# Corner clears moved from Pool to VectorE, output stores moved from SyncE to ScalarE, in a fused attention and expert-layer kernel

## The chip, the cores and the metric

The kernel runs on one core of a Trainium2 chip. The metric is the device time of one execution in microseconds (us). "Span" is the length of one execution inside its trace; it is about 1.8 us shorter than the time.

Each core has TensorE (matmuls; its weight loads are listed apart as PEld), VectorE (DVE), ScalarE (ACT), GpSimd (POOL) and SyncE (SP, which here only issues DMA transfers). Each gets its own list of instructions, and the timelines below show them carried out in that order.

## The reference

Causal block attention over 8 batches, 8 heads, 576 positions of width 64, with blocks of 64; then an expert layer with an activation that has a parameter for each hidden column.

```python
def _attn_ref(q, k, v):                       # (8, 8, 576, 64) each
    scores = scale * np.matmul(q, k.transpose(0, 1, 3, 2))
    # ... mask: a query's block of 64 sees its own block and the earlier ones
    attn = np.exp(scores - max)               # cut
    attn = attn / (np.sum(attn, axis=-1, keepdims=True) + 1e-09)
    return np.matmul(attn, v)

def _moe_ref(x, w_in, w_out, beta):           # x (4608, 512), w_in (512, 2048), w_out (2048, 512)
    h = x @ w_in
    g = h * (1.0 / (1.0 + np.exp(-beta * h)))
    return g @ w_out
```

## The kernel before

The kernel doesn't write its instructions down in order. It hands operations to a small planner: engine, assumed duration in ns, function that emits it, what it depends on, which buffers it uses, and a priority. The planner simulates the engines with those durations and so fixes one order for each engine; then semaphores are given out and each engine's list is emitted. An operation that changes its engine, or its assumed duration, can therefore change the order of everything.

```python
P.schedule()          # list scheduling: fixes P.order["PE"], ["ACT"], ["DVE"], ["POOL"], ["SP"]
P.assign(None)        # semaphores
# ...
def emit(self, e, eng, sems):
    for o in self.order[e]:
        for n, v in o.waits:
            eng.wait_ge(sems(n), v)           # the whole queue of the engine stands here
        ins = o.emit(eng, e)
        # ...
```

A pair of heads makes three large exponentials on ScalarE, and after each one a 64x64 corner that the causal mask forbids has to be set to zero in both heads. Scores are stored with the key on the partition axis, so a corner lies in partitions 64 to 127. Attention times V waits for these clears.

```python
x = P.op("ACT", act_t(1024), fe, deps=[o], tiles=[ps, te], ...)       # exponential, line 560
def fz(g, e, g0=g0, te=te):
    if g0 < 2:
        return g.memset(E3[te.slot][64:128, g0, :, 0:64], 0.0)        # line 566, 64 times
    # ... the third one: two corners in each head
    return g.memset(bass.AP(...), 0.0)                                # line 568, 32 times
zs.append(P.op("POOL", 200, fz, deps=[x], tiles=[te], prio=-40))
# ...
av = P.op("PE", 30 * 34, fav, deps=ex + zs + [load[u]], ...)          # attention times V, line 595
```

Pool also casts V of a batch from float32 to bf16 (line 441, `Vn<-Vs`), casts Q and K (lines 484 and 523), and issues the loads of `w_in` (line 396) and `w_out` (line 401), all in one queue. SyncE issues the loads of Q, K and V (V is lines 427 and 430), the transposing transfers (lines 530 and 625), and the stores:

```python
x = P.op(("ACT", "DVE"), 600, fv2, deps=[o], tiles=[po, to], lat=680, prio=0)      # scale by 0.5, line 722
def fd(g, e, to=to, row=row, w=w):
    return [g.dma_start(out[row + 128 * w:row + 128 * w + 128, :], ost[to.slot][:])]  # line 728
P.op("SP", 400, fd, deps=[x], tiles=[to], xfer=900, dma=["d_ost", to], prio=0)
```

The expert layer is lines 680 (matmuls of the first layer), 690 (tanh), 694 (multiply) and 711 (matmuls of the second layer), in nine chunks of 512 tokens. While the first scores aren't there yet, TensorE runs throwaway matmuls (line 411).

The softmax here doesn't subtract the row's maximum and nothing guards it: scores larger than these inputs give would overflow.

## Time and profile before

| | before |
|---|---|
| time, median of the first 3 runs | 370.88 us (369.81 to 371.85) |
| span of the profiled run | 369.8 us, mean granted TensorE clock 0.995 |
| busy: TensorE / ScalarE / VectorE / Pool | 343.9 / 209.1 / 156.6 / 96.8 us |

The views that show what bounds the kernel stand in the prediction, with their reading. The groups of the two clears on Pool (count, busy time, mean ns of one, then Pool's idle time ahead of them), and the row of the stores among the DMA issues (size, then us from issue to landing):

```profile
L566 POOL MEMSET E<- 64x128 bf16 x64 | 13.1, 205 | 85.9 <-ACT E L560 83.8
L568 POOL MEMSET E<- 64x256 bf16 x32 | 9.8, 307 | 37.3 <-ACT E L560 36.1
...
out_dram<-ost SPq DMA_DIRECT2D x36, 256.0 KB, 2.2
```

96 clears are 23 us of work, in front of which Pool stands 123 us. And the busy time by engine in the two microseconds after the wait for the V cast that the prediction points at; the number after the engines is the granted clock:

```profile
56.00:58.00 2.00, 2.00 (x41) 2.00 (x38) 0.32 (x3) 0.00 (x0) 0.31 (x2) 0.50 1.21 195
```

TensorE is counted as fully busy there, at half speed.

### The profile page before, as it was taken

To read this page: it belongs to the slowest core of one execution; us is meant where nothing else is said; L and a number is where in the kernel's file an instruction comes from. 1 tells how busy PE (TensorE), PEld (TensorE's weight loads), DVE (VectorE), ACT (ScalarE), POOL (GpSimd) and SP (SyncE) were. 2 spreads that over 40 slices of the span, in tenths; PEclk is the share of its full clock that TensorE was granted. 3 is DMA by queue.
4 is the path that set the end of the run, shared out by engine and by line. 5 is a ranking of instruction groups with operands and counts; after the bars stand their busy time and mean duration, and the time that the engine had idled before them with its cause. 6 is when DMAs were issued, how large, how long until landed. Compare 5 with 4: busy or idle time off the path is not lost.

```text
span 369.8 us, 6994 instructions
## 1 busy us (share of the span) xinstructions
PE 343.9 (93%) x2755; PEld 176.0 (48%) x2797; DVE 156.6 (42%) x342; ACT 209.1 (57%) x308; POOL 96.8 (26%) x198
## 2 busy tenths in 40 slices
PE   7979969999898898998999999899999999999986
PEld 5656527544444544554544444345544444444432
DVE  1565954056412664325751246215631730730710
ACT  1573793138627788539875599219823832733711
POOL 6565173103605606405505331501000000000000
PEclk9999998999999999999999999999999999999999
DMA  8999999198898998998968799582112002002002
GB/s 194 220 190 268 205 188 152 43 214 195 173 231 201 203 191 188 208 222 197 194 125 183 190 183 202 124 160 76 32 46 86 1 30 79 6 30 83 2 30 85
DMA packets 146529, 52.06 MB, mean 141 GB/s; under 512 B 134704, under 2 KB 141888, under 8 KB 146496
## 3 DMA queue, kind: packets, MB, share of 16 engines
q1 hardware_dynamic: 139872, 46.82, 56.8%
q0 software_dynamic: 4224, 4.19, 7.1%
q10 hardware_dynamic: 2400, 0.59, 0.9%
q8 instruction: 22, 0.36, 0.4%
q14 instruction: 11, 0.09, 0.1%
HBM read 36.71 MB, written 9.44 MB: 125 GB/s over the span
## 4 chain that ended last, share of the span: by engine, by line
PE 78%; ACT 12%; DVE 4%; issue 3%; POOL 2%; POOLq 0%
PE PS L711 34%; PE PS L680 28%; ACT E L560 8%; PE PS L595 7%; ACT th L690 3%; PE PS L552 3%; PE PS L411 3%; DVE gT L694 2%; PE PS L637 2%; POOL Vn L441 1%; DVE xq L613 1%; ACT ost L722 1%; PE PS L493 1%; ACT E L572 0%; DVE xT L644 0%
## 5 line engine op out<-in xcount | busy, mean ns | idle before, releaser
L694 DVE SCALAR_TENSOR_TENSOR gT<-th,PS 128x512 bf16<-128x512 f32 x144 | 97.5, 685 | 105.8 <-ACT th L690 105.5
L680 PE MATMUL PS<-xT,w_in 128*128 128x512 bf16 x554 | 127.8, 379 | 3.0 <-DVE xT L644 0.6
L711 PE MATMUL PS<-w_out,gT 128*128 128x512 bf16 x556 | 125.8, 379 | 4.2 <-DVE gT L694 2.6
L690 ACT ACTIVATE th<-PS,beta 128x512 f32<-128x512 f32 x144 | 98.7, 707 | 33.8 <-PE PS L680 33.8
L560 ACT ACTIVATE E<-PS 128x1024 bf16<-128x1024 f32 x96 | 96.0, 1061 | 18.0 <-PE PS L552 17.8
L711 PEld LDWEIGHTS PS<-w_out,gT 128*128 128x128 bf16 x576 | 54.9, 98 | 68.6 <-DVE gT L694 3.7
L680 PEld LDWEIGHTS PS<-xT,w_in 128*128 128x128 bf16 x576 | 53.2, 98 | 64.8 <-DVE gT L694 2.1
L722 ACT ACTIVATE ost<-PS 128x512 f32<-128x512 f32 x35 | 20.9, 597 | 101.9 <-PE PS L711 101.9
L552 PE MATMUL PS<-QKT 64*64 64x64 bf16 (+5 forms) x384 | 36.9, 281 | 5.3 <-ACT E L560 3.7
L595 PE MATMUL PS<-Vn,E 128*128 128x65 bf16 x960 | 35.6, 196 | 5.4 <-POOL Vn L441 2.2
L523 POOL CAST QKn<-ST 128x640 bf16<-128x640 f32 x48 | 34.6, 721 | 14.6 <-DMA ST<-in_k_dram 7.4
L595 PEld LDWEIGHTS PS<-Vn,E 128*128 128x128 bf16 x960 | 32.8, 99 | 11.3 <-issue 3.4
L566 POOL MEMSET E<- 64x128 bf16 x64 | 13.1, 205 | 85.9 <-ACT E L560 83.8
L605 DVE RECIPROCAL inv<-PS 128x5 f32<-128x5 f32 x64 | 8.3, 173 | 49.1 <-PE PS L595 49.0
L613 DVE TENSOR_TENSOR xq<-PS,inv 128x320 bf16<-128x320 f32 x64 | 28.5, 486 | 0.0
L552 PEld LDWEIGHTS PS<-QKT 64*128 64x128 bf16 (+1 forms) x384 | 13.5, 95 | 29.9 <-issue 11.2
L441 POOL CAST Vn<-Vs 128x2560 bf16<-128x2560 f32 (+1 forms) x9 | 18.7, 2082 | 22.2 <-DMA Vs<-in_v_dram 21.5
L644 DVE COPY xT<-PS 128x64 bf16<-128x64 bf16 (+2 forms) x44 | 10.7, 287 | 29.2 <-PE PS L637 29.2
L568 POOL MEMSET E<- 64x256 bf16 x32 | 9.8, 307 | 37.3 <-ACT E L560 36.1
L411 PE MATMUL PS<-identF,identB 128*128 128x256 bf16 x104 | 15.8, 310 | 2.2 <-POOL identF L355 2.2
L501 DVE COPY QKT<-PS 128x576 bf16<-128x576 bf16 x16 | 11.7, 752 | 8.3 <-PE PS L493 8.3
L411 PEld LDWEIGHTS PS<-identF,identB 128*128 128x128 bf16 x104 | 10.9, 111 | 5.1 <-POOL identF L355 2.2
(29 smaller groups left out, 63.6 us busy)
## 6 DMA issues: line engine op xcount, KB each, us to landing
out_dram<-ost SPq DMA_DIRECT2D x36, 256.0 KB, 2.2
Vs<-in_v_dram SPq DMA_DIRECT2D x28, 256.0 KB, 4.0
ST<-in_q_dram SPq DMA_DIRECT2D x48, 128.0 KB, 2.8
ST<-in_k_dram SPq DMA_DIRECT2D x48, 128.0 KB, 2.7
ST<-in_q_dram SPq DMA_DIRECT2D x8, 288.0 KB, 7.9
ST<-in_k_dram SPq DMA_DIRECT2D x8, 288.0 KB, 7.9
w_in<-in_moe_w_in_dram POOLq DMA_DIRECT2D x4, 512.0 KB, 6.8
w_out<-in_moe_w_out_dram POOLq DMA_DIRECT2D x4, 512.0 KB, 9.3
```

The source lines that it names most:

```text
L411: return g.matmul(PS[:, tf.slot, 0:256], identB[:], identW)
L441: return g.tensor_copy(Vn[t.slot][:, :, h0:h1, 0:64], Vs[ts.slot][:, :, h0:h1, :])
L523: return g.tensor_copy(QKn[tn.slot][:].rearrange("p a w n -> p (a w n)")[:, 640 * (2 * a + w):][:, 0:640] .rearrange("p (t h d) -> p t h d ...
L552: z = g.matmul(o, QKT[tqk.slot][r, p, 1, 128 * t:128 * t + m], QKT[tqk.slot][r, p, 0, q0:q1])
L560: return g.activation(E3[te.slot][:, g0, :, :], PS[:, ps.slot:ps.slot + 2, :], ACT.Exp, scale=0.125)
L595: z = g.matmul(o, eblk(te, t, i, h), Vn[Tv.slot][:, t, 2 * c + h, 0:65], start=(t == 0), stop=(t == i))
L613: return g.tensor_tensor(xq[tx.slot][:, :, 64 * w:64 * w + 64], a, x, ALU.mult)
L680: z = g.matmul(PS[:, ph.slot, :], w_in[:, c, 128 * j:128 * j + 128], xT[:, c, row % RX:row % RX + RC], start=(c == 0), stop=(c == 3))
L690: return g.activation(th[tt.slot][:], PS[:, ph.slot, :], ACT.Tanh, scale=beta[:, j:j + 1])
L694: return g.scalar_tensor_tensor(out=gT[tg.slot][:, j, :], in0=th[tt.slot][:], scalar=1.0, in1=PS[:, ph.slot, :], op0=ALU.add, op1=ALU.mult)
L711: z = g.matmul(PS[:, po.slot, :], gT[tg.slot][:, j, 128 * w:128 * w + 128], w_out[:, j, :], start=(j == 0), stop=(j == NJ - 1))
L722: return g.activation(ost[to.slot][:], PS[:, po.slot, :], ACT.Copy, scale=0.5)
```

## The change

Its intent: Pool and SyncE each carry a kind of instruction that mostly waits for ScalarE, and everything behind it in the same in-order queue waits along. The clears go to VectorE. The scaling of an output tile goes to ScalarE always, and ScalarE then issues the store itself.

```diff
-                    zs.append(P.op("POOL", 200, fz, deps=[x], tiles=[te], prio=-40))
+                    zs.append(P.op("DVE", 160 if g0 < 2 else 220, fz, deps=[x], tiles=[te], prio=-20))
 ...
-                x = P.op(("ACT", "DVE"), 600, fv2, deps=[o], tiles=[po, to], lat=680, prio=0)
+                x = P.op("ACT", 600, fv2, deps=[o], tiles=[po, to], lat=680, prio=0)
 ...
-                P.op("SP", 400, fd, deps=[x], tiles=[to], xfer=900, dma=["d_ost", to], prio=0)
+                P.op("ACT", 500, fd, deps=[x], tiles=[to], xfer=900, dma=["d_ost", to], prio=-1)
```

## The prediction

> **What bounds the kernel now.** I read the engine table first, then the stages (busy time in chosen stretches), then the waits of every engine and of the SyncE queue, and last the instructions in order of time around the gaps of TensorE.
>
> ```profile
> PE 343.9 (93%) x2755; PEld 176.0 (48%) x2797; DVE 156.6 (42%) x342; ACT 209.1 (57%) x308; POOL 96.8 (26%) x198
> DMA  8999999198898998998968799582112002002002
> ```
> TensorE is the bound: 343.9 of 369.8 us, 25.9 us idle. The DMA row shows a second limit: the 16 DMA engines are full for about the first 60 us.
>
> ```profile
> 0.00:32.00 32.00, 27.50 (x341) 19.80 (x342) 15.42 (x41) 13.17 (x17) 17.93 (x49) 1.00 1.07 212
> 32.00:60.00 28.00, 24.35 (x216) 13.24 (x218) 17.91 (x32) 19.64 (x29) 12.78 (x21) 0.94 1.12 207
> 270.00:350.00 80.00, 79.63 (x365) 36.32 (x371) 30.82 (x45) 37.96 (x57) 0.00 (x0) 1.00 0.12 42
> ```
> The columns are the stretch, its length, busy time of TensorE, its weight loads, VectorE, ScalarE and Pool, granted clock, DMA share and GB/s. The idle time is not even: 4.5 us before 32, 3.65 us in 32 to 60, 12.7 us in 60 to 270 (the attention and the expert layer interleaved), 0.4 us in the 80 us of expert layer alone. The last 19.8 us hold 4.7, of which about 3 are the last scaling and store. The group of throwaway matmuls of the fill (104, 15.8 us in records that overlap; their starts are 0.11 us apart) hides another 11 us of emptiness before 32 us. So only the first 270 us can give anything, and at most some 35 us.
>
> ```profile
> POOL E L566 <- ACT E L560: 83.8, 40, 9.4
> POOL E L568 <- ACT E L560: 36.1, 23, 9.5
> PEld PS L595 <- POOL E L568: 0.8, 3, 0.3
> SPq L728 <- ACT ost L722: 110.5, 21, 18.9
> ```
> These are waits: total, times, longest. Pool stands 120 us before the corner memsets, and the SyncE queue 110 us before the output stores. But TensorE waits for a memset itself only 0.8 us. Any gain must therefore come from what stands behind them in the same in-order queues.
>
> ```profile
> 10.15 0.82 POOL L484 CAST QKn<-ST 96x768 bf16<-96x768 f32 x1 [2.28 <-DMA ST<-in_k_dram]
> 13.95 0.20 POOL L566 MEMSET E<- 64x128 bf16 x1 [2.98 <-ACT E L560]
> 14.49 0.87 POOL L396 DMA_DIRECT2D w_in<-in_moe_w_in_dram  x1 [0.34 <-POOL E L566]
> ...
> 18.59 0.82 POOL L484 CAST QKn<-ST 96x768 bf16<-96x768 f32 x1
> ...
> 46.19 0.20 POOL L566 MEMSET E<- 64x128 bf16 x1 [8.26 <-ACT E L560]
> ...
> 53.17 0.20 POOL L566 MEMSET E<- 64x128 bf16 x1 [1.18 <-ACT E L560]
> 53.43 2.32 POOL L441 CAST Vn<-Vs 128x2560 bf16<-128x2560 f32 x1
> ```
> This is Pool in order of time; the bracket is the idle time before. Two harms are visible. The K of the third head pair was issued at 3.6 us and landed 9.1 us later, at 12.7, yet is cast at 18.59: the weight load was issued late, behind a memset, and casts queue behind both. ScalarE then idles 2.13 us until the third pair's scores (its exponential starts at 21.54). And batch 1's V was issued by 43.3 us and had landed by 46.6, yet is cast at 53.43, behind memsets.
>
> ```profile
> 55.80 3.42 PE L595 MATMUL PS<-Vn,E 128*128 128x65 bf16 x60 [2.25 <-POOL Vn L441]
> ```
> TensorE pays 2.25 us for it, and then runs these 60 matmuls in 3.42 us where 30 take 1.01 us elsewhere; the granted clock of 55.8 to 59.3 is 0.54. That is another 1.4 us.
>
> **What the Trainium skill says.** "VectorE: DVE Perf Modes", section on zero memsets, states that a memset takes one cycle per element whatever the type. The trace agrees for float32: VectorE's own 64x256 memset takes 272 ns, against 267 for 256 cycles of 0.96 GHz. "SBUF — State Buffer", section "Who interferes with whom", says that a VectorE instruction with at most one SBUF input outside the 2-port modes doesn't contend with GpSimd; the trace of before cannot test it for these memsets. "DMA: Bandwidth & Descriptors", "Issuing engines are not separate DMA queues", says issuing from more engines saves only the sequencer's issue time, since the same 16 engines move the data. "Perfetto Trace Analysis", "DMA Instruction — HWDGE", puts the semaphore wait on the issuing sequencer ahead of the issue: the wait is what holds SyncE here, 110.5 us, where an issue itself takes 0.36 us in the median.
>
> **The change part by part.**
>
> Memsets. Pool loses 64 of 205 ns and 32 of 307 ns, 13.1 + 9.8 = 22.9 us, and with them the 120 us of waiting. VectorE gains, by one cycle per element (an estimate from the page above and the 272 ns row), 64 x 0.14 + 32 x 0.27 = 17.6 us: 156.6 becomes 174 us, 47%. It is far from a bound. The memset still follows its exponential, now in VectorE's queue, where it can meet a 0.69 us multiply (row 694) in front. As VectorE's multiplies follow ScalarE's tanh, in ScalarE's own order, a memset waiting for an exponential blocks little that could have run. I set +0.3 us.
>
> Pool freed, first stretch: the K cast can run near its landing, so the third pair's scores can follow the second's. I take the 2.1 us idle of ScalarE as gained; the first expert matmul (31.98 us, after the fourth pair's last copy) comes that much earlier. -2.1 us.
>
> Pool freed, 53 to 59: the V cast could run from 46.6 and end before 49. Removable are 2.25 + 1.4 = 3.65 us. The DMA engines are full here, and w_out issued earlier competes with V, so I credit three quarters: -2.8 us.
>
> Stores. SyncE loses 36 issues and the 110 us. The longest block is 18.9 us, from 53 to 71.85: the remaining V of batch 2 is issued at 73.95 and 79.98 and Pool waits 17.4 us for it, while DMA is at a 0.29 share in 60 to 70. TensorE does not idle then, having expert work (29.16 of 30 us in 60 to 90). The benefit can come only later, in the 12.7 us idle of 60 to 270, whose named waits are mainly on exponentials and multiplies, not loads. I credit an eighth: -1.5 us.
>
> ScalarE gains 36 issues. Its own queue issued four loads in 2.16 us at the start, 0.54 us each: 36 x 0.54 = 19 us, invisible as busy time. It must also wait for its own scaling to complete before the store. Twelve fall after 270 us, where it is busy 37.96 of 80 us: free. Of the other 24 only those in stretches where ScalarE is full count (10.00 of 10 us in 210 to 220): at most four, of which half meet a wait for TensorE. 2 x 0.54, +1.0 us. One scaling that VectorE did (679 ns) goes to ScalarE (597 ns): nothing.
>
> End: the last scaling ends at 367.26, SyncE issues at 367.28, the span ends 2.5 us later. ScalarE issuing it itself changes at most 0.1 us.
>
> Sum: +0.3 - 2.1 - 2.8 - 1.5 + 1.0 = -5.1 us, 370.88 - 5.1 = 365.8 us.
>
> **The rivals.** (a) The first 60 us belong to DMA: share 1.07 and 1.12. Then earlier casts only meet later data, and w_out and V trade places; the gain there falls to about 1 us and the time is 369. Against it: both named late casts had data waiting for 6 us. (b) The kernel plans its instruction order at build time from assumed durations, so the change reorders everything. If Pool, SyncE and their loads stay close to plan, the gaps at 93 to 97, 113 to 123 and 140 to 145 us, where attention runs without expert work between, could close as well: half of 12.7 us gives another 5, about 360. For it: batch 2's scores start only at 88.7 us, after 27 us almost without attention. Against it: TensorE's order is a plan's result, and the plan never saw these blocks. (c) ScalarE becomes the bound of the mixed stage: 99 of 145 us busy in 125 to 270 plus stores and their waits. If every one of the 24 stores delayed an exponential by 0.6 us that TensorE waits for, 14 us would be added and the time would be 375 or more. The 101.9 us that scalings wait for TensorE speak against it. (d) VectorE blocks: a memset in its queue that waits for an exponential holds the reciprocals and copies of the previous pair, and TensorE's chain turns around more slowly: +3 us, 369.
>
> **Range and chances.** My sum has large uncertain credits, and a new plan alone can move some microseconds either way. The range is 360.5 to 370.5 us, with (b) at the low end and (a) or (d) at the high one. The 2% line is 363.5 us: 2.3 us below my figure, within reach of (b): chance of faster 0.34. Within 2%: 0.60. Slower than 378.3 needs (c) in full or a bad plan: 0.06.
>
> **What would show it.** Right: Pool's waits for exponentials gone, about 72 to 75 us busy; the third pair's exponential near 19.4 us; first expert matmul near 30 us; no TensorE wait for the V cast near 53 and no clock near half there; SyncE's wait for scalings gone and no DMA hole at 60 to 70; 80 us of expert work alone unchanged near the end; VectorE near 174 us. Wrong: new TensorE waits on VectorE memsets, ScalarE stretches at 100% holding stores with TensorE idle beside them, memset rows longer than 0.3 us, or a first expert matmul still at 32 us. If the gain lies mostly in 60 to 270 us, rival (b) was the real mechanism and my two head terms were not.

## The result, and the profile after

| | before | after |
|---|---|---|
| median of 4 runs each | 370.35 us (369.29 to 371.85) | 366.76 us (366.54 to 367.03) |
| ratio | | 0.990, 95% interval 0.986 to 0.994: the same, by the 2% line |
| span of the profiled run, clock | 369.8 us, 0.995 | 364.7 us, 1.000 |

A ratio is the mean time of one kernel's fast runs over that of the other's in the same rounds, so it is not quite the ratio of the medians.

The kernel is faster by about 1%, and its runs scatter less. The engine rows:

```profile
PE 346.0 (95%) x2797; PEld 174.3 (48%) x2797; DVE 169.7 (47%) x437; ACT 209.2 (57%) x309; POOL 74.4 (20%) x102
```

(The 2.1 us more that TensorE seems to be busy can be a matter of records: in the trace of before 42 of its 2797 matmuls are missing, as its row in the prediction shows.) The stages, to be laid beside those of before:

```profile
0.00:32.00 32.00, 26.59 (x337) 19.30 (x338) 17.50 (x52) 13.17 (x17) 15.38 (x37) 1.00 1.10 222
32.00:60.00 28.00, 26.56 (x265) 13.84 (x264) 21.14 (x50) 22.09 (x32) 11.93 (x14) 1.00 1.14 204
270.00:350.00 80.00, 78.50 (x365) 35.44 (x363) 30.86 (x45) 37.41 (x56) 0.00 (x0) 1.00 0.11 40
```

The first stage has not gained. The second has TensorE busy 2.2 us longer at full clock instead of 0.94.

A better ruler than stages is how far TensorE has come. The expert matmuls have 1152 weight loads (9 chunks of 128), all of them in both traces. Reading the start of the n-th one in each trace and subtracting gives a ledger: where it steps, time was gained or lost.

```
n-th weight load of the expert matmuls   before     after     after - before
0                                          31.98     32.35      +0.37
64                                         59.84     57.15      -2.69
128                                        78.25     75.60      -2.65
384                                       164.69    162.00      -2.69
512                                       205.88    203.19      -2.69
576                                       228.71    225.37      -3.34
640                                       246.31    240.78      -5.52
736                                       274.78    269.67      -5.11
1151 (the last)                           366.03    360.92      -5.11
```

(Between the 384th and the 512th the two kernels run attention and expert work in another order, so the difference swings there and comes back.) Two steps make the whole gain: 3.06 us between 32 and 60 us, and 2.4 us between 205 and 275 us. Nothing was gained in the first 32 us, and nothing in the 145 us between the steps.

**The first step.** Pool's cast, then the first matmuls that use it (the x30 are one head pair; a bracket would show idle time before them), then the stretch with TensorE's clock:

```profile
51.11 2.32 POOL L441 CAST Vn<-Vs 128x2560 bf16<-128x2560 f32 x1 [9.28 <-DMA Vs<-in_v_dram]
```
```profile
53.64 1.08 PE L595 MATMUL PS<-Vn,E 128*128 128x65 bf16 x30
```
```profile
56.00:58.00 2.00, 2.00 (x30) 1.13 (x27) 2.00 (x8) 1.10 (x2) 0.23 (x1) 1.00 1.02 204
```

V of batch 1 is cast at 51.11 instead of 53.43 us, and attention times V follows its scores without idle time. The 2.25 us wait and the half clock after it are gone together. Note the bracket: Pool now waits 9.28 us for V to land. Before, the data was there and Pool was late; now Pool is early and the data sets the time. The data itself comes later than before: the last part of this V lands at 51.05 instead of 46.58 us, though it is issued at the same time (43.2 us). What changed ahead of it is that Pool, freed, issues three `w_out` loads at 39.6 to 41.1 us, where they went out at 48.7 to 50.7. So of the 6.85 us for which V lay ready before its cast, the change gains 2.3. That the loads are the cause isn't tried by itself; in vcast_early below they go out from 48.41 us on, and V lands at 45.92.

**The second step.** Before, then after: SyncE's issue of the first part of batch 7's V and, later, of a pair of transposing transfers (`xT<-xq`), and two of the attention groups of TensorE.

```profile
218.80 1.23 SPq L427 DMA_DIRECT2D Vs<-in_v_dram  x2
...
231.14 2.56 SPq L625 DMA_TRANSPOSE xT<-xq  x2
...
234.93 1.06 PE L595 MATMUL PS<-Vn,E 128*128 128x65 bf16 x30 [0.87 <-issue]
...
240.44 1.06 PE L595 MATMUL PS<-Vn,E 128*128 128x65 bf16 x30 [0.99 <-issue]
```
```profile
212.84 1.21 SPq L427 DMA_DIRECT2D Vs<-in_v_dram  x2
...
224.38 3.06 SPq L625 DMA_TRANSPOSE xT<-xq  x2
...
230.56 1.07 PE L595 MATMUL PS<-Vn,E 128*128 128x65 bf16 x30
...
234.92 1.07 PE L595 MATMUL PS<-Vn,E 128*128 128x65 bf16 x30
```

The V transfer is issued 6.0 us earlier, 3.3 us more than the lead that TensorE already had, and two idle stretches of TensorE of 0.87 and 0.99 us are gone. The view doesn't say what these matmuls waited for before ("issue"), but the landings do: before, pairs of `xT<-xq` land at 234.84 and 240.35 us, and the two groups start 0.09 us after each; after, they land at 228.59 and 234.10, and the groups at 230.56 and 234.92 don't wait. In the code an attention group takes an `xq` buffer that such a transfer must have read, and in clear_oldplan below the trace names this wait for the same group. So the second step comes through SyncE's transposing transfers. That stores held them up is what both_oldplan shows against clear_oldplan: the stores alone are moved there, and the wait is gone.

**The waits.** Total, times and longest:

```profile
POOL Vn L441 <- DMA Vs<-in_v_dram: 99.1, 9, 28.8
DVE E L566 <- ACT E L560: 31.1, 36, 7.4
```

Pool's waits for exponentials are gone; it now waits for data. VectorE does wait for exponentials, but as part of the same time in which it waited for other things before. SyncE's 110.5 us before the stores are gone as well: the longest wait of its queue is now the closing one for the last stores to land, 99.2 us at the end of its list, where it has nothing else to do.

**The new instructions.** The clears on VectorE, the landing of the stores, and the group of scalings on ScalarE:

```profile
L566 DVE MEMSET E<- 64x64 uint32 x64 | 7.2, 112 | 33.3 <-ACT E L560 31.1
L568 DVE MEMSET E<- 64x128 uint32 x32 | 5.3, 165 | 18.5 <-ACT E L560 17.3
...
out_dram<-ost ACTq DMA_DIRECT2D x36, 256.0 KB, 2.4
```

The build turned a zero memset of 128 bf16 values into one of 64 uint32 values. They cost 12.5 us in all.

**The first 32 us.** Pool, then ScalarE's third pair, then VectorE. The last fence is TensorE's transposes of the third pair, before and then after:

```profile
11.29 2.37 POOL L396 DMA_DIRECT2D w_in<-in_moe_w_in_dram  x3
14.06 1.25 POOL L441 CAST Vn<-Vs 128x1280 bf16<-128x1280 f32 x1 [0.40 <-DMA Vs<-in_v_dram]
15.37 2.09 POOL L484 CAST QKn<-ST 96x768 bf16<-96x768 f32 x2
...
23.75 1.25 POOL L441 CAST Vn<-Vs 128x1280 bf16<-128x1280 f32 x1 [5.60 <-DMA Vs<-in_v_dram]
```
```profile
21.14 1.94 ACT L560 ACTIVATE E<-PS 128x1024 bf16<-128x1024 f32 x2 [2.02 <-PE PS L552]
```
```profile
19.20 0.17 DVE L568 MEMSET E<- 64x128 uint32 x1 [0.52 <-ACT E L560]
...
19.58 0.72 DVE L501 COPY QKT<-PS 128x576 bf16<-128x576 bf16 x1
```
```profile
19.47 0.68 PE L493 MATMUL PS<-identB,QKn 96*128 96x96 bf16 x12 [0.39 <-POOL QKn L484]
...
20.35 0.43 PE L493 MATMUL PS<-identB,QKn 96*128 96x96 bf16 x6 [1.12 <-DVE QKT L501]
```

The K of the third pair is cast 3.2 us earlier (from 15.37 instead of 18.59), as foreseen, and yet the third pair's exponential starts at 21.14 instead of 21.54 us, hardly more than the 0.29 us by which ScalarE's first exponential came earlier (12.52 for 12.81). The first line of the last fence says why so little was there: before, TensorE waited only 0.39 us for that cast, because the transposes stand in its own queue behind the second pair's 30 attention matmuls, which ended at 19.08 us. After, they run at 18.55 us without a wait, and TensorE then waits 1.12 us for VectorE's copy. Two things stand in the way now. VectorE waits 0.52 us for an exponential before a clear, with the copy of the third pair's K behind it. And Pool, no longer held by clears, issues three of the four `w_in` loads from 11.29 us on and the fourth at 17.41, where it was two from 14.49 and two at 20.87; the second half of batch 0's V lands behind them, at 23.70 instead of 18.86 us, and is cast at 23.75 instead of 22.39.

### The profile page after: what moved, and what is told of

Its sections match the earlier page's. It is cut to its first block, busy times and chain, and to the rows that moved or that the text cites. A ratio compares the mean times of both kernels' runs of the same rounds, so it can differ in the third digit from the quotient of the medians.

```text
span 364.7 us, 6938 instructions
## 1 busy us (share of the span) xinstructions
PE 346.0 (95%) x2797; PEld 174.3 (48%) x2797; DVE 169.7 (47%) x437; ACT 209.2 (57%) x309; POOL 74.4 (20%) x102
## 4 chain that ended last, share of the span: by engine, by line
PE 74%; ACT 14%; DVE 3%; issue 1%
PE PS L711 34%; PE PS L680 28%; ACT E L560 8%; PE PS L595 6%; ACT th L690 5%; PE PS L552 3%; DVE gT L694 2%; PE PS L637 2%; ACT ost L722 1%; PE PS L411 1%; ACT E L572 1%; DVE xq L613 0%; DVE xT L644 0%; DVE inv L605 0%; PE PS L493 0%
## 5 line engine op out<-in xcount | busy, mean ns | idle before, releaser
L680 PE MATMUL PS<-xT,w_in 128*128 128x512 bf16 x576 | 132.4, 380 | 1.1 <-DVE xT L644 0.6
L711 PE MATMUL PS<-w_out,gT 128*128 128x512 bf16 x576 | 128.0, 379 | 2.7 <-DVE gT L694 2.7
L595 PE MATMUL PS<-Vn,E 128*128 128x65 bf16 x960 | 34.4, 193 | 2.6 <-DVE gT L694 2.0
L595 PEld LDWEIGHTS PS<-Vn,E 128*128 128x128 bf16 x960 | 31.5, 97 | 7.9 <-DVE gT L694 2.5
L566 DVE MEMSET E<- 64x64 uint32 x64 | 7.2, 112 | 33.3 <-ACT E L560 31.1
L568 DVE MEMSET E<- 64x128 uint32 x32 | 5.3, 165 | 18.5 <-ACT E L560 17.3
```

Source lines behind the costliest of these rows:

```text
L595: z = g.matmul(o, eblk(te, t, i, h), Vn[Tv.slot][:, t, 2 * c + h, 0:65], start=(t == 0), stop=(t == i))
L680: z = g.matmul(PS[:, ph.slot, :], w_in[:, c, 128 * j:128 * j + 128], xT[:, c, row % RX:row % RX + RC], start=(c == 0), stop=(c == 3))
L711: z = g.matmul(PS[:, po.slot, :], gT[tg.slot][:, j, 128 * w:128 * w + 128], w_out[:, j, :], start=(j == 0), stop=(j == NJ - 1))
```

## The experiments

All twelve are timed in five rounds against the kernel before on the same chip, all gave correct results, and all are "same" by the 2% line; the interesting differences are below it. "Old plan" means that the planner ran on the kernel before and the named operations were moved to another engine's list afterwards, at the place that their planned start gives them; so the order within each engine stays as it was. "Re-planned" means that the planner saw the change. The ledger gives the lead over the kernel before at the 0th, 64th, 544th and last weight load, in us, from one profiled run each.

| run | edit | median us | ratio (95%) | ledger |
|---|---|---|---|---|
| after | both, re-planned | 366.76 | 0.990 (0.986 to 0.994) | +0.37 / -2.69 / -2.81 / -5.11 |
| clear_oldplan | clears, old plan | 368.76 | 0.995 (0.991 to 0.999) | -0.83 / -3.67 / -3.60 / -1.49 |
| store_oldplan | stores, old plan | 370.60 | 0.997 (0.993 to 1.002) | +0.16 / +0.23 / +0.24 / -0.92 |
| both_oldplan | both, old plan | 367.01 | 0.991 (0.987 to 0.994) | -0.01 / -2.87 / -2.80 / -4.61 |
| clear_only | clears, re-planned | 368.05 | 0.991 (0.987 to 0.995) | +0.19 / -2.86 / -3.26 / -2.99 |
| store_only | stores, re-planned | 372.67 | 1.001 (0.996 to 1.006) | profile slow |
| oldengines_newplan | after's order, before's engines | 371.26 | 1.001 (0.998 to 1.005) | -0.20 / -2.51 / -2.51 / +0.22 |
| vcast_early | before, one cast moved | 367.39 | 0.991 (0.988 to 0.993) | -0.31 / -3.72 / -3.72 / -4.04 |
| vcast_store | that and the stores, old plan | 365.71 | 0.986 (0.983 to 0.990) | +0.22 / -3.17 / -2.88 / -3.94 |
| w_in_late | after, two `w_in` loads later | 366.81 | 0.989 (0.986 to 0.992) | +0.52 / -2.54 / -2.66 / -4.40 |
| v_first | after, all `w_in` loads later | 367.96 | 0.991 (0.988 to 0.995) | -0.08 / -2.71 / -2.80 / -4.69 |
| copy_first | after, one clear behind a copy | 366.28 | 0.987 (0.984 to 0.990) | -0.21 / -3.26 / -3.35 / -5.41 |
| v_and_copy_first | the last two together | 368.46 | 0.992 (0.988 to 0.995) | -1.19 / +0.19 / +0.07 / -1.46 |

A word on the first column of the ledger: the second K cast of the head starts anywhere between 9.5 and 10.5 us in these traces, because its transfer lands so. Half a microsecond at the 0th load is landing, not the edit.

The theory going in: the gain is queues that no longer stand in front of ready work (Pool's at 53 us, SyncE's late in the run). The rival: the planner's new order made it.

### clear_oldplan and store_oldplan: each part alone, order kept

```diff
         P.schedule()
+        for name, e in (("fz", "DVE"),):           # store_oldplan: (("fd", "ACT"),)
+            for o in P.ops:
+                if o.emit.__name__ == name and o.eng != e:
+                    P.order[o.eng].remove(o); P.order[e].append(o); o.eng = e
+        for e in P.order:
+            P.order[e].sort(key=lambda o: o.start)
```

> The plan of the kernel before is kept; afterwards only the 96 corner memsets are moved from Pool's list to VectorE's, at their planned place. Theory A (a freed Pool casts batch 1's V in time, a freed SyncE brings the last batches' loads and transposes in time): the lead over the kernel before is 2.7 to 3.1 us after the 64th expert matmul (near 57 us) and stays there to about 205 us; nothing or little is added after 205 us; in all -2.5 to -3.5 us, about 367.5 us. Rival B (the new instruction order of TensorE makes the gain): the order is the old one, so at most -0.5 us. Rival C (the memsets in VectorE's queue hold up its copies): a loss of 0.3 to 1 us before 32 us, as in the changed kernel.

> The plan of the kernel before is kept; afterwards only the 36 output stores are moved from SyncE's list to ScalarE's, at their planned place. Theory A: no lead before 205 us (TensorE still waits for batch 1's V cast, 2.2 us near 53 us), then -2 to -2.5 us between 205 and 246 us, about 368.3 us. Rival B (new order makes the gain): 0 within 0.5 us. Rival D (the stores burden ScalarE): +1 us or more in 205 to 225 us.

With the clears alone the first step is there in full (2.8 us between the 0th and the 64th), and then 2.1 us is lost late, in front of a group of attention times V that waits for a transposing transfer:

```profile
232.61 1.07 PE L595 MATMUL PS<-Vn,E 128*128 128x65 bf16 x30 [1.99 <-DMA xT<-xq]
233.73 5.09 PE L711 MATMUL PS<-w_out,gT 128*128 128x512 bf16 x15
```

Fifteen matmuls in 5.09 us, where sixteen take 3.62 us elsewhere: the clock is below 1 again after the idle time. This run is not typical in that: it took 370.18 us against a median of 368.76, and the other five kept a mean clock of 1.000. With the stores alone the first step is absent, wait and half clock included, and 1.2 us come late:

```profile
55.97 3.48 PE L595 MATMUL PS<-Vn,E 128*128 128x65 bf16 x60 [2.25 <-POOL Vn L441]
```

So in the traces the clears make the first step and the stores act late, each where the theory has it. The late part is half of the 2 to 2.5 us expected, and the timed runs don't show it: 370.60 us against 370.56 for the kernel before in the same rounds.

### both_oldplan and oldengines_newplan: engines or order?

both_oldplan is the edit above with both pairs of names. oldengines_newplan is the reverse: after's plan, with the clears put back on Pool and the stores on SyncE.

```diff
         P.schedule()
+        # as above, on the kernel after:
+        for name, e in (("fz", "POOL"), ("fd", "SP")):
```

> Plan of the kernel before; memsets moved to VectorE's list and stores to ScalarE's afterwards. The memsets alone gave -3.6 us by the 64th expert matmul and lost 2.1 us of it between 220 and 237 us, where TensorE waited 2 us for a transpose that SyncE had issued late. Theory A (SyncE, held by the stores, is what takes the lead back): -3.6 at 57 us, kept past 237 us, -4.5 us (-3.8 to -5.2) at the end, about 366.3 us, more than the sum of the two alone (-1.5 and -0.9). Rival B (the changed kernel's new order of TensorE made its late gain): the lead falls again to about -1.5 to -2.4 us at the end, 368.5 us.

> The changed kernel's plan and TensorE order, but memsets put back into Pool's list and stores into SyncE's. Theory A: the V cast of batch 1 is late again (TensorE waits 2 us or more between 50 and 60 us), SyncE waits some 100 us for scalings; the end is within -1 us of the kernel before. Rival B (order): -2 us or more of late gain stays.

Both parts in the old order give 367.01 us, nearly all of the gain; the new order with the old engines gives nothing, 371.26 us. The rival falls as an account of the whole gain. The last ledger column leaves 0.5 us to the order late in the run (-4.61 against -5.11), one profile each, below what the timed runs can tell.

oldengines_newplan showed something else. It also leads by 2.3 us at the 64th load, with the V cast at 52.36 and an idle time of 1.75 us, after which the clock stays 1.00; so in this profile an order that just escapes the half clock has most of the first step too. It then gives everything back at one place:

```profile
217.49 0.26 PE L552 MATMUL PS<-QKT 64*64 64x64 bf16 x2 [2.65 <-DMA QKT<-QKn]
217.68 1.89 PE L680 MATMUL PS<-xT,w_in 128*128 128x512 bf16 x4
```
```profile
219.00:222.00 3.00, 3.00 (x10) 0.67 (x10) 0.69 (x1) 1.63 (x3) 0.20 (x1) 0.50 1.29 239
```

Four expert matmuls take 1.89 us instead of 1.04 us: half clock again, after 2.65 us of idle time.

### clear_only and store_only: each part alone, planned

These are the first hunk and the other two hunks of the diff.

> The first part of the change alone, planned anew. Theory A: -2.7 to -3.1 us from 53 to 59 us, TensorE never waits for a V cast there; the SyncE queue still waits about 110 us for scalings and the late part gives nothing or up to -1 us by a new order; 367 to 368 us. Rival B: the late gain of about 2.4 us shows here if the order from about 165 us on is the changed kernel's.

> The second part of the change alone, planned anew. Theory A: TensorE's wait for batch 1's V cast and the low granted clock near 56 us stay, the SyncE queue doesn't wait for scalings, 2 to 2.5 us come between 205 and 246 us: 368 to 369 us. Rival B: a time near the changed kernel's only if its order of TensorE is the same.

The clears alone, planned, give 368.05 us with SyncE's wait before the stores still at 112.9 us. The stores alone give nothing: their re-planned run still has the 2.25 us wait for the V cast. One could take from this that stores are worthless; but on top of the clears they are worth 1.8 us in the old plan (368.76 against 367.01, medians from different rounds) and 1.3 us planned (368.05 against 366.76). The intervals of the ratios overlap in both pairs, so timing alone doesn't settle it. The traces side with it: clear_oldplan waits 1.99 us for a transposing transfer at 232 us, and both_oldplan doesn't wait there.

### vcast_early: one instruction

If the gain at 53 us is only that Pool's cast comes late, then moving that one cast must give it, with every clear still on Pool. On the kernel before:

```diff
         P.schedule()
+        pool = P.order["POOL"]
+        cast = [o for o in pool if o.emit.__name__ == "fw"][2]       # V of batch 1
+        last = [o for o in pool if o.emit.__name__ == "fwo"][3]      # the fourth w_out load
+        pool.remove(cast)
+        pool.insert(pool.index(last) + 1, cast)                      # was two clears later
```

> The kernel before with one Pool instruction moved: batch 1's V cast runs right after the last issue of w_out (about 51.4 us) and ahead of two corner memsets, not behind the one that waits for its exponential at 53.2 us. Theory A: TensorE's second-layer attention matmuls of batch 1 start near 54.1 in place of 55.8 us, the idle time before them falls from 2.25 to about 0.5 us and the granted clock does not drop: -1.7 us without and -3.1 us with the clock's part at the 64th expert matmul. At the end -1 to -2 us, as SyncE's late transposes take part of it back. Rival (V's data or DMA is what is late): no change.

```profile
51.15 2.32 POOL L441 CAST Vn<-Vs 128x2560 bf16<-128x2560 f32 x1
...
53.52 1.98 PE L595 MATMUL PS<-Vn,E 128*128 128x65 bf16 x60 [0.28 <-POOL Vn L441]
```

367.39 us, a ratio of 0.991, the same as the whole change's 0.990, and all six runs kept a mean clock of 0.999 or more. Sixty matmuls take 1.98 us instead of 3.42. Two clears in front of one cast account for all that the first half of the change gains at this place.

### vcast_store: the change's gain without its first half

The cast moved as above, and the stores moved to ScalarE in the old plan.

> The kernel before with two edits: batch 1's V cast moved ahead in Pool's list (alone: -3.7 us at 57 us, -4.0 at the end), and the stores moved from SyncE to ScalarE (alone: -0.9 us at the end, all of it between 220 and 237 us). The memsets stay on Pool. If the whole gain of the change is these two waits, this kernel equals the changed one without moving a memset: -3.7 us at 57 us and -4.5 to -5 us at the end, 365.9 to 366.9 us, with the clock at 1.00. If the memsets on VectorE matter by themselves, it stays at -4 us or less.

365.71 us, the lowest median of all, with mean clock 1.000 in all six runs. Its profiled run was its slowest (span 365.9; the other five lie between 363.5 and 364.3), so its ledger understates it. It is about 1 us below the change by medians; the intervals of the two ratios overlap, so that it beats the change isn't shown, only that it does at least as well with all 96 clears left on Pool.

### w_in_late, v_first, copy_first, v_and_copy_first: why the head gained nothing

The prediction had 2.1 us there. Two suspects are in the traces above: `w_in` loads ahead of V, and the clear ahead of the copy. All four kernels start from the kernel after.

```diff
+        # w_in_late: the third and fourth w_in load behind batch 0's second V cast
+        # v_first: all four w_in loads behind the first V cast and the K casts of pairs 3 and 4
+        # copy_first: on VectorE, one clear (the one at 19.20) behind the copy of pair 3's K
+        # v_and_copy_first: v_first and copy_first together
```

> The changed kernel with the third and fourth loads of w_in issued after the second half of batch 0's V is cast, not at 13.6 and 17.4 us. If the earlier weight load is what held the head back (share of the DMA engines over 1, V's second half landing at 23.7 us): V lands 1 to 2 us earlier, and the first expert matmul comes 0.4 to 0.8 us earlier relative to the first K casts. If VectorE's order is (memsets waiting for an exponential ahead of a copy near 19 us): no earlier than 0.2 us. The later loads may be missed by expert matmuls 8 to 15 of the first chunk, which would add idle time near 36 to 40 us.

> The changed kernel with all four loads of w_in issued after batch 0's first V cast and the K casts of pairs three and four (from about 15.5 us, not 11.3), so behind the loads of V's second half. Theory (w_in's first loads take V's bandwidth in the changed kernel): V's second half lands within 7 us of its issue, near 20 us and not 23.7, and the third pair's attention matmuls no longer wait for a V cast (0.58 us). First expert matmul 0.2 to 0.6 us earlier after the second K cast (21.8 us in both kernels). Rival (VectorE's order alone sets it): no change of that distance. Batch 1's loads wait for w_in and may come 1 us later, so the end is unlikely to move by more than 0.5 us.

> The changed kernel with one memset (second pair, third exponential) put behind the reciprocals and the copy of the third pair's K on VectorE, where it had waited 0.5 us for its exponential ahead of them. If VectorE's in-order wait is what held the third pair back: that copy starts at 18.9 to 19.1 us and not 19.58, the third pair's exponential 0.4 to 0.8 us earlier after the first (8.6 us in both kernels). The first expert matmul gains less than 0.4 us, as V's second half then limits.

> Both edits to the changed kernel. If the two limits stand one behind the other, the first expert matmul comes 0.7 to 1.2 us earlier after the second K cast than in the changed kernel (21.8 us), more than the sum of the two alone; the 64th expert matmul is at most 0.5 us earlier if batch 1's V is then the limit. End: 366.0 to 366.8 us.

To keep the landing of the head's transfers out of it, times here are counted from the start of the second K cast. The first expert matmul comes 21.83 us after it in the kernel before as well as after.

w_in_late missed: the V half was cast 13.00 us after the K cast against 13.23, and the first expert matmul came at 22.90. I had moved the wrong pair; the first two loads are the ones ahead of V. v_first took all four away, and V's second half was then cast 9.81 us after the K cast without a wait for data, but the first expert matmul gained only 0.12 us. copy_first brought the third pair's exponential to 8.10 us after the first one (8.62 in the kernel after, 8.73 before), and the first expert matmul still came at 21.97, as V's second half was late as ever (4.79 us wait for data, cast 13.37 us after the K cast). With both mended it came at 21.09 us, 0.74 less. That would be two limits in parallel, where taking one away shows nothing, but it rests on one profile each: kernels whose head is that of the kernel before (vcast_early, vcast_store, store_oldplan) lie between 21.82 and 22.32 us, and clear_oldplan, whose third exponential also comes 8.10 us after the first and whose V is nearly as late (12.84 us), has 21.43. And even with both mended ScalarE idles 1.50 us before the third pair, against 2.13 in the kernel before.

And that 0.74 us was given back with more. With the `w_in` loads late, the last part of batch 1's V is issued at 44.58 instead of 43.21 us and lands at 53.48 instead of 51.05, with the DMA share at 1.2 from 50 to 56 us, and the old loss at 53 us is there again:

```profile
53.53 2.32 POOL L441 CAST Vn<-Vs 128x2560 bf16<-128x2560 f32 x1 [10.54 <-DMA Vs<-in_v_dram]
...
55.90 3.08 PE L595 MATMUL PS<-Vn,E 128*128 128x65 bf16 x60 [3.75 <-POOL Vn L441]
```

In this kernel, putting one of the head's transfers earlier put another later, at a place that cost more.

### The clock as a bistable cost

The clock records in the packed traces are finer than the windows above. Leaving out the end of the run, where TensorE is done, each stretch at half clock lasts 3.41 us (6.83 in oldengines_newplan), and the stretches at full clock between are whole multiples of that: 47.79 us in the kernel before is 14 of them, 358.4 us in the kernel after 105. So each trace gives a grid of windows of 3.41 us. It doesn't start with the kernel: the first full clock comes between 5.2 and 8.3 us. Put together, TensorE's idle stretch, how long it was busy in the window of the grid around it, and the clock in the next window:

| kernel, place | idle us | busy, of 3.41 us | clock in the next window |
|---|---|---|---|
| vcast_early, 53 us | 0.28 | 2.74 | 1.00 |
| v_first, 54 us | 1.27 | 2.22 | 1.00 |
| oldengines_newplan, 54 us | 1.75 | 1.79 | 1.00 |
| clear_oldplan, 232 us | 1.99 | 1.37 | 0.50 |
| before, 55 us | 2.25 | 0.97 | 0.50 |
| store_oldplan, 55 us | 2.25 | 0.79 | 0.50 |
| oldengines_newplan, 217 us | 2.65 | 1.30 | 0.50 |
| v_and_copy_first, 55 us | 3.75 | 0.54 | 0.50 |

In the twelve fast profiles that hold clock records, the full-clock windows between 15 and 350 us part cleanly: those in which TensorE was busy for 1.37 us or less are followed by half clock, and those with 1.78 us or more are not. The clock came back after half-clock windows that were busy for 3.21 us or more, and not after the one with 2.88 (in oldengines_newplan). (clear_only's trace holds no such records; store_only's profile, slow, has one exception, at 2.05.) Whether 2.25 us of idle time falls into one window or is split between two depends on the grid of that run. No experiment varied it by itself, and some matmul records are missing, so the two limits are rough.

The 33 runs of the kernel before beside the experiments fall into groups by their mean clock: 12 runs at 0.999 or more with a mean span of 368.0 us, 17 at 0.994 to 0.995 with 369.7, 4 at 0.991 with 370.8. One window at half clock loses at most half of 3.41 us, 1.7 us; by mean clock and span the groups have none, one and two. So the kernel before has such an episode in most runs, but not in all. All four runs of the kernel after have 0.999 or more, with a mean span of 364.95. Against the full-clock runs of before that is 3.0 us; against all 33 (mean 369.2 us) it is 4.3, though these ran in other rounds. The difference, 1.2 us, goes with the clock, which also fits the smaller scatter of the kernel after.

## Why the prediction was right or wrong

The predicted time was 365.8 us and the measured one 366.76; the class and the range hold. The profiles' lead, 5.11 us, even equals the predicted sum of 5.1. That is luck in part: two of its terms were off by about 2 us, in opposite directions. (The profiled run of before took 371.59 us, more than three of its four timed runs; the timed medians differ by 3.6 us, not 5.1.)

- **"Pool freed, 53 to 59", -2.8 us: right.** Measured 3.06 us, wait and half clock gone together. vcast_early shows the mechanism by itself: one cast moved ahead of two clears gives this step. The quarter held back for `w_out` against V was well placed: V landed 4.5 us later than before.
- **"Pool freed, first stretch", -2.1 us: this step failed.** The K cast did come 3.2 us earlier, but the third pair's exponential came at 21.14 us and not near 19.4, and the first expert matmul at 32.35, not near 30. The prediction took ScalarE's whole idle stretch of 2.13 us for removable because one of the things in the chain before it was late. The trace of before shows that TensorE waited only 0.39 us for that cast: its own queue reached the third pair's transposes at 19.08 us. With the cast early, ScalarE still idles 2.02 us. Behind the cast stand a clear in VectorE's queue ahead of the copy (rival (d), small) and, for the first expert matmul, `w_in` ahead of V in the DMA queues (rival (a)). Mending both gives 0.74 us at the first expert matmul in one profile, not 2.1, and it is taken back at 53 us.
- **Stores, "an eighth: -1.5 us", with +1.0 us for ScalarE and +0.3 us for clears in VectorE's queue: right in kind, mis-sized in sum.** Net -0.2 us was predicted for everything after 60 us; measured -2.4 us, all of it after 205 us. From the 544th load to the end, the stores alone give -1.2 us in the old plan (and -1.1 in vcast_store, where vcast_early without them has -0.3); with the clears moved as well -1.8; in the new order -2.3. So the credit was near, and the two costs taken off it weren't to be seen: an issue on ScalarE takes 339 ns in the median, not the 540 ns taken from the loads at the start, and TensorE idles beside only one of the 36 (0.92 us at 111 us), where the kernel before idles as long without a store. What the stores held up late was SyncE's transposing transfers, not only loads. The prediction's longest block, 18.9 us, is one that gave nothing. SyncE had issued all of batch 2's V by 67.5 instead of 81.9 us, the DMA share in 60 to 90 us rose from 0.61 to 1.01, and TensorE's lead did not change between 60 and 205 us.
- **Clears, 17.6 us on VectorE: over-sized**, 12.5 us, as they came out as uint32. VectorE's busy time is 169.7 us instead of the estimated 174. Nothing depended on it.
- **Pool 72 to 75 us, the 80 us of expert work unchanged, the tail unchanged: right.** Pool is at 74.4 us; the ledger is flat at -5.11 from the 736th load to the end.
- **Rival (b), a new order closes the gaps at 93 to 145 us: wrong.** The ledger is flat there, and both_oldplan gives nearly all the gain without a new order. **Rival (a), data that comes later once the casts are early: partly right**, in the head and at batch 1's V, but the gain at 53 us stayed. **Rival (c), ScalarE as a bound: wrong**, though it is at 10.00 of 10 us in 210 to 220 after as before.

The sentence of the prediction that if the gain lay mostly in 60 to 270 us rival (b) was the mechanism turned out too simple: nearly half of it lies there, and the cause is the engines, not the order.

## What to carry to other kernels

In an in-order queue, look for an instruction that waits and costs little (a clear, a store) in front of one that is ready and feeds the bound; then try to move only the ready one ahead, as a single moved cast did here what 96 moved clears do. Where several things end an engine's idle time together, credit a removal only with the distance to the next of them, and ask which transfer is made later by the one that is made earlier. And keep a ledger of the bounding engine's progress against the old kernel: a sum that comes out right can hide two terms that don't.

## What the Trainium skill lacked or had wrong

- "TensorE: Matmul & The Clock Gate", Part 1, says the gate has two states, half and full clock, and falls to half after an idle window of about 3.4 us, the windows running freely; its section "Why this matters for your kernels" advises no gaps above about 3 us between bursts. The two states (0.50 and 1.00), the window (3.41 us) and its free running agree with the traces. What it lacks is how idle a window must be: TensorE was still busy for 0.54 to 1.37 us in the windows that led to half clock, with idle stretches of 1.99 us and more, so the advised 3 us are not safe; 1.78 us of busy time kept the full clock. That 12 of 33 runs of the same kernel kept it fits windows that run freely; only the profiled runs have the record to show it.
- "VectorE: DVE Perf Modes", section on zero memsets, says that a zero memset of bf16 can be issued as uint32, with half the elements. The prediction used only its first half, one cycle per element. What the section lacks is that this build does it by itself, and the fixed part: 64 words take 112 ns and 128 words 165 ns, so 0.83 ns a word and some 59 ns beside, by the profile's rows. That is less than the 1.04 ns of a cycle at the prediction's 0.96 GHz, and it gives the 272 ns of 256 words as well; the agreement that the prediction saw there is no support for one cycle per element.
- "SBUF — State Buffer", "Who interferes with whom", agrees: with 96 clears on VectorE, Pool's casts of Q and K (line 523) take 720 ns in the mean against 721 before, the 14 of 48 that overlap a clear included.
- No page that I read says what a cheap waiting instruction costs what stands behind it in an engine's queue. Here two clears of 0.2 to 0.3 us in front of one cast cost 3.4 us of TensorE's progress (vcast_early, 0th to 64th load, half clock included), and 110.5 us of SyncE's waits before stores cost 1.1 to 2.3 us in the traces.
